# Softcap attention and a gated feed-forward layer: a fourth PSUM bank for the values, six early weight units, and a new order at the end of the first stage

## Chip, core and metric

The kernel runs on one NeuronCore of a Trainium2 chip. The metric is the device time of one execution in microseconds (us); the time given is the median of several executions. One execution was also profiled, and every row shown below comes from that one.

## What is computed

The input is an attention layer over 4 batches, 12 heads, 448 positions and 64 columns per head, with a cap on the scores, followed by a gated feed-forward layer over the 1792 rows that the attention gives (768 columns inside, 1536 in the middle). Everything is float32; the feed-forward weights arrive as 64-bit floats.

```python
scores = scale * np.matmul(q, k.transpose(0, 1, 3, 2))
scores = cap * np.tanh(scores / cap)
attn = np.exp(scores - np.max(scores, axis=-1, keepdims=True))
attn = attn / (np.sum(attn, axis=-1, keepdims=True) + 1e-09)
x = np.matmul(attn, v)                 # 4 x 12 x 448 x 64, then 1792 x 768
gate = 1.0 / (1.0 + np.exp(-(x @ w_gate)))
out = (gate * (x @ w_val)) @ w_out
```

## The kernel before

**Attention.** Heads are worked on in pairs: 24 pairs, six to a batch. For pair n the program transposes K and Q on TensorE (`tp`, L208), splits the result into a high and a low part (`T`: high by ScalarE, L175, low by VectorE, L181), multiplies them into four chunks of scores (`sc`, L323, six matmuls of each), takes the tanh of each chunk (ScalarE, L326) and one exp per head (L334). The values are multiplied in pair n+1's turn, one head at a time (`emit_PV`, tiles `pv`, L364, four matmuls of 448 columns each for one head). For the first twelve pairs ("direct") the row sums come out of the same matmuls, as a second half of the `pv` tile. ScalarE copies them into `rd` (L389, one buffer), and VectorE does the normalisation: it adds an epsilon (L413), takes the reciprocal (L414), and multiplies (L417, two instructions, which for the first six pairs read `pv` straight from PSUM). The result `xraw` is then split for the feed-forward layer into `xspl`, one slot per pair (`flush_x`: high by GpSimd, L173, low by GpSimd in batch 0 and by VectorE later, L181).

**PSUM.** There are eight banks: two tiles of two banks for scores and transposes (`ps_s`), one bank `ps_v`, and three banks `ps_m`. In the first stage, in which the first six pairs run with no feed-forward work beside them (`alone`), all `pv` tiles take turns in the three banks of `ps_m`, and `ps_v` lies unused. A pair needs two `pv` tiles, so the second one of a pair needs a bank that the pair before has just used, and which is free only when both L417 of that pair are done. From pair 6 on `pv` tiles use `ps_v`, and `ps_m` holds the feed-forward sums.

**Weights.** The feed-forward weights are 36 units of 768 KB: 0 to 23 are columns of w_gate and w_val in turns of four, 24 to 35 are rows of w_out. Each is loaded raw (L594), converted by one ScalarE (L611) and three VectorE instructions (L612 to L614) and split into high (L175 on ScalarE, or L173 on GpSimd for an early unit) and low (L181 on VectorE); the split unit `wspl` is written to memory (`wd`, L650) for the later batches. `o.early` units are converted in the first stage, in the order 3, 4, ..., 0, 1, 2, at a pace set by how much attention has been done (L819); the early ones from 3 on are loaded back when they are needed (L662). The others are converted in batch 0 of the feed-forward layer, unit u+4 when unit u begins.

**Feed-forward.** For each batch (`moe`): 24 tiles `h` (L706, 18 matmuls of 448 columns over six slots of `xspl`, in order of the slots, so the last three need pair 5 of the batch), then the output `o` (L782). While batch b's feed-forward work runs, the attention of batch b+1 is woven in: TensorE and ScalarE follow the program's order, and the loop at L826 hands out pieces of one or the other so that the done shares stay level, against a total of 570 for the feed-forward side (`tot_m`). The pieces of one batch's feed-forward work add up to 617 by their own weights (432 for the `h` tiles, 185 for the `o` tiles), so the attention of a batch is over before the feed-forward work is. On VectorE, GpSimd and the DMA queue of SyncE a scheduler sets the order when the program is built, by priority, which is program order unless a block raises it.

At the end of the first stage (n = 6, `last`), the loop L430 runs pair 6's first two score chunks, both heads' values of pair 5, pair 5's normalisation, and then leaves the stage; pair 6's other two chunks, pair 7's transposes and scores come as woven work:

```python
        for late in range(2):
            if (late == 0) != last and live:
                yield emit_S(n, 2) + emit_S(n, 3)
                emit_T(n + 1)
```

Of the kernel before, what the change touches and what calls it, by code (L numbers as in the profile page):

```python
# [20 lines left out]
EPS = 1e-9  # L21
WARM = 10
BANK = 512
NCH = 4

# [5 lines left out]
def tile_softcap_attention_then_gated_ffn(  # L31
# [33 lines left out]
    c["v0"] = c["pair0"][:, 2 * n0:].rearrange("p (c d) -> p c d", d=q.shape[3])  # L65
    _load_inside(nc.sync, c["qk0"][:, 1], k, 0)
    _load_inside(nc.scalar, c["qk0"][:, 0], q, 0)
    _load_evenly(nc, c["v0"], v, 0)
# [30 lines left out]

def _load_inside(eng, t, src, n):  # L100

    s = _pair(src, n)
    for h in range(2):
        eng.dma_start(
            out=t[0:src.shape[2] // NCH, :, h, :], in_=s[h].rearrange("(c p) d -> p c d", c=NCH)
        )
# [41 lines left out]
class _Ops:  # L148
# [37 lines left out]
    def load_qk(self, n, evenly=False):  # L186

        if n >= self.B * self.NPAIR:
            return None
        qk = self.ap.tile([P, 2, NCH, 2, self.D], F32, tag="qk", bufs=2, name=f"qk{n}")  # L190
        if evenly:
            _load_inside(self.nc.sync, qk[:, 1], self.k, n)
        else:
            _load_k(self.nc, qk[:, 1], self.k, n)
        _load_inside(self.nc.sync, qk[:, 0], self.q, n)
        return qk
# [18 lines left out]
def _bounded_attention(o, x_done):  # L215
# [14 lines left out]
    nc, c, ap = o.nc, o.c, o.ap  # L230
    o.early = 10
    o.out_tag = ("v_spl", 2)
# [123 lines left out]
    def emit_PV(n, j):  # L356
        if alone(n):
            pv = o.ps_m.tile([P, S], F32, tag="m", name=f"pv{n}_{j}")
        else:
            pv = o.ps_v.tile([P, S], F32, tag="v", name=f"pv{n}_{j}")  # L360
# [38 lines left out]
    def emit_out(n):  # L399
        b, p = divmod(n, o.NPAIR)  # L400
        xr = row(n)
        if direct(n):
            rd = rds.pop(n)
        else:
            ps = o.two_banks(f"dn{n}")[:, 0, 0:S]
            for j in range(2):
                nc.tensor.matmul(
                    ps, ones[:, (1 - j) * D:(3 - j) * D], Asum.pop((n, j)), start=(j == 0),
                    stop=(j == 1),
                )  # L410
            rd = ap.tile([P, S], F32, tag="rd", bufs=1, name=f"rd{n}")
            nc.scalar.activation(rd, ps, AF.Copy)
        nc.vector.scalar_tensor_tensor(rd, rd, EPS, rd, ALU.mult, ALU.add)  # L413
        nc.vector.reciprocal(rd, rd)  # L414
        if alone(n):
            for j in range(2):
                nc.vector.tensor_mul(xr[half(j)], pvs.pop((n, j))[0:D], rd[half(j)])  # L417
        else:
            nc.vector.tensor_mul(xr, xr, rd)
        x_done(b, p, x_raw[b])  # L420

# [6 lines left out]
    for n in range(NP + 1):  # L428
# [3 lines left out]
        if n > 0:  # L432
# [3 lines left out]
            if not direct(n - 1):  # L436
                emit_P(n - 1, 1)
        for late in range(2):

            if (late == 0) != last and live:  # L440
                yield emit_S(n, 2) + emit_S(n, 3)
                emit_T(n + 1)
                if n + 2 < NP:
                    qks[n + 2] = o.load_qk(n + 2, direct(n + 2))
                yield 5
                emit_exp(n, 0)
                if not direct(n):
                    emit_P(n, 0)
            if late != last and n > 0:
                yield from emit_PV(n - 1, 1)  # L450
# [4 lines left out]
                yield 2  # L455
                vs.pop(n - 1)
                if n % o.NPAIR == 0:
                    yield None
                load_v(n + 1)
        if not live:  # L460
# [87 lines left out]
def _emit(tc, ctx, c, attention_of, q, k, v, w_gate, w_val, w_out, out):  # L548
# [265 lines left out]
    with tc.manual_schedule(engines=MS):  # L814
# [6 lines left out]
        for b in range(B):  # L821
            m = moe(b)
            done_m, done_a, tot_m, tot_a = 0, 0, 570, H * o.head(b + 1)
            live_a = b + 1 < B
# [44 lines left out]
```

## Time and profile before

| | |
|---|---|
| median of 3 runs | 808.39 us (807.21 to 809.38) |
| the profiled execution | 810.49 us |
| its span, first to last instruction | 808.7 us |
| TensorE busy | 761.1 us (94%) |
| VectorE busy | 463.5 us (57%) |
| ScalarE busy | 398.1 us (49%) |
| GpSimd busy | 200.8 us (25%) |
| granted TensorE clock, mean | 0.972 |

The time of an execution is the span and a little around it (1.79 us here). Busy shares are means over very different stages: the first stage ends at about 104 us, feed-forward batch 0 at about 296 us, and the end of the span has no attention in it. Clock 1.0 is 2.4 GHz, 0.5 is 1.2 GHz.

### The profile page before, as it was taken

How to read it: one execution, taken by the hardware profiler on the slowest of the kernel's cores; microseconds unless marked ns; L12 is line 12 of the kernel's file. 1: busy time of each engine (PE TensorE's matmuls, PEld its weight loads, DVE VectorE, ACT ScalarE, POOL GpSimd, SP SyncE). 2: the span in 40 equal slices, each digit the busy share in tenths (PEclk: the TensorE clock that was granted, in tenths of full speed). 3: DMA queues.
4: the chain of work that ended last, by engine and by line, in shares of the span. 5: the costliest groups of instructions: out<-in, count | busy, mean ns of one | idle time of the engine just before them, and what ended most of it. 6: DMA issues, size and time to landing. Idle time of an engine off the chain costs nothing.

```text
span 808.7 us, 10161 instructions
## 1 busy us (share of the span) xinstructions
PE 761.1 (94%) x3908; PEld 647.6 (80%) x3908; DVE 463.5 (57%) x519; ACT 398.1 (49%) x417; POOL 200.8 (25%) x215
## 2 busy tenths in 40 slices
PE   7988789999998989999999999999998999999993
PEld 5544468878777878898889898889898999999993
DVE  1699803769798972865788545677688101211000
ACT  5787446676865654757574428565852020110000
POOL 1233301002030050634355322445363000100000
PEclk8999989999999998999999999999999999999997
DMA  9599675688999994566557776454469866665531
GB/s 224 155 291 285 201 234 160 204 259 276 346 307 300 351 286 144 183 194 188 171 184 228 246 246 194 167 184 156 157 192 272 284 245 219 232 211 200 174 110 53
DMA packets 133745, 176.14 MB, mean 218 GB/s; under 512 B 86200, under 2 KB 111288, under 8 KB 133688
## 3 DMA queue, kind: packets, MB, share of 16 engines
q1 hardware_dynamic: 132760, 175.17, 67.6%
q8 instruction: 33, 0.54, 0.3%
q10 hardware_dynamic: 928, 0.23, 0.1%
q14 instruction: 24, 0.20, 0.1%
HBM read 138.41 MB, written 36.18 MB: 216 GB/s over the span
## 4 chain that ended last, share of the span: by engine, by line
PE 73%; DVE 12%; ACT 5%; POOL 4%; issue 3%; DMA 1%; SPq 0%; POOLq 0%; DVEq 0%; ACTq 0%
PE h L706 39%; PE o L782 17%; PE pv L364 6%; PE sc L323 6%; DVE rd L414 3%; PE pv L373 2%; PE pv L374 2%; PE tp L208 1%; DVE pl L181 1%; POOL xspl L173 1%; ACT ph L175 1%; ACT gate L744 1%; DVE rd L413 1%; PE tp L294 1%; DVE ph L181 1%
## 5 line engine op out<-in xcount | busy, mean ns | idle before, releaser
L706 PE MATMUL h<-xspl,wspl 128*128 128x448 f32 x1728 | 380.2, 374 | 10.9 <-POOL xspl L181 6.5
L706 PEld LDWEIGHTS h<-xspl,wspl 128*128 128x128 f32 x1728 | 323.5, 189 | 53.7 <-issue 14.2
L782 PE MATMUL o<-wspl,gspl 128*128 128x384 f32 x864 | 161.2, 339 | 3.3 <-DVE osb L795 1.9
L782 PEld LDWEIGHTS o<-wspl,gspl 128*128 128x128 f32 x864 | 150.5, 188 | 9.4 <-issue 3.5
L326 ACT ACTIVATE t<-sc,scale 112x896 f32<-112x896 f32 (+1 forms) x96 | 91.2, 1001 | 25.5 <-PE sc L323 25.0
L173 POOL TENSOR_SCALAR gspl<-gate 128x448 fp32r<-128x448 f32 x48 | 39.2, 816 | 222.9 <-DVE gate L740 222.9
L364 PE MATMUL pv<-t,vo 112*128 112x448 f32 x192 | 86.3, 586 | 5.7 <-DVE xraw L417 5.7
L738 ACT ACTIVATE gate<-h 128x448 f32<-128x448 f32 x48 | 25.9, 542 | 124.0 <-PE h L706 98.4
L334 ACT ACTIVATE t<-t,capv 112x1792 f32<-112x1792 f32 (+1 forms) x48 | 85.6, 1788 | 0.4
L323 PE MATMUL sc<-T 64*112 64x448 f32 (+1 forms) x576 | 75.6, 392 | 5.2 <-ACT T L175 2.0
L323 PEld LDWEIGHTS sc<-T 64*112 64x112 f32 (+1 forms) x576 | 49.9, 183 | 30.8 <-issue 12.4
L414 DVE RECIPROCAL rd<-rd 128x448 f32<-128x448 f32 x24 | 70.8, 2948 | 0.4
L740 DVE TENSOR_TENSOR gate<-h,gate 128x448 f32<-128x448 f32 x48 | 29.3, 611 | 68.9 <-PE h L706 68.8
L364 PEld LDWEIGHTS pv<-t,vo 112*128 112x128 f32 x192 | 37.9, 204 | 36.1 <-issue 31.0
L181 DVE TENSOR_TENSOR T<-tp,T 128x896 fp32r<-128x896 f32 (+1 forms) x24 | 26.8, 1118 | 58.2 <-ACT T L175 58.2
L346 POOL TENSOR_TENSOR a<-t 128x448 f32<-128x448 f32 x24 | 29.8, 1243 | 117.2 <-ACT t L334 102.1
L797 ACT ACTIVATE osb<-o 128x384 f32<-128x384 f32 x8 | 3.9, 491 | 101.8 <-PE o L782 89.0
L795 DVE COPY osb<-o 128x384 f32<-128x384 f32 x16 | 8.7, 551 | 71.7 <-PE o L782 71.6
L181 DVE TENSOR_TENSOR pl<-t,ph 128x1344 fp32r<-128x1344 f32 x24 | 46.3, 1928 | 4.3 <-ACT ph L175 4.2
L175 ACT ACTIVATE ph<-t 128x1792 fp32r<-128x1792 f32 x24 | 40.7, 1696 | 14.3 <-PE pv L375 11.3
L175 ACT ACTIVATE T<-tp 128x896 fp32r<-128x896 f32 (+1 forms) x24 | 22.7, 944 | 43.2 <-PE tp L208 43.2
L181 DVE TENSOR_TENSOR gspl<-gate,gspl 128x448 fp32r<-128x448 f32 x48 | 31.3, 653 | 17.4 <-POOL gspl L173 16.6
(68 smaller groups left out, 758.8 us busy)
## 6 DMA issues: line engine op xcount, KB each, us to landing
wspl<-wd SPq DMA_DIRECT2D x115, 768.0 KB, 4.4
wd<-wspl SPq DMA_DIRECT2D x36, 768.0 KB, 6.4
w<-in_moe_w_gate_dram SPq DMA_DIRECT2D x12, 768.0 KB, 5.2
w<-in_moe_w_val_dram SPq DMA_DIRECT2D x12, 768.0 KB, 7.1
w<-in_moe_w_out_dram SPq DMA_DIRECT2D x12, 768.0 KB, 7.2
qk<-in_q_dram SPq DMA_DIRECT2D x46, 112.0 KB, 4.3
out_dram<-osb SPq DMA_DIRECT2D x8, 576.0 KB, 6.4
qk<-in_k_dram SPq DMA_DIRECT2D x22, 112.0 KB, 3.9
```

Source lines behind the costliest of these rows:

```text
L173: self.nc.gpsimd.tensor_scalar(dst, src, 1.0, 1.0, ALU.mult, ALU.mult)
L175: self.nc.scalar.activation(dst, src, AF.Copy)
L181: e.tensor_sub(dst, src, hi.bitcast(F32))
L323: nc.tensor.matmul(ps[0:w, j, 0:S], a[rows], r[rows], start=(i == 0), stop=(i == len(ops) - 1))
L326: nc.scalar.activation(Pt[n][0:w, :, m, :], ps[0:w, :, 0:S], AF.Tanh, scale=c["scale"][0:w])
L334: nc.scalar.activation(t, t, AF.Exp, scale=c["cap"][rows])
L346: nc.gpsimd.tensor_add(a, t[:, 0, :], t[:, 1, :])
L364: nc.tensor.matmul(pv, vs[n][0:QC, j * NC + m, :], Pt[n][0:QC, j, m, :], start=(m == 0), stop=(m == NC - 1),)
L414: nc.vector.reciprocal(rd, rd)
L706: nc.tensor.matmul(ps, a, r, start=(kk == 0 and i == 0), stop=(kk == KD - 1 and i == 2))
L740: nc.vector.tensor_mul(gt, ps, gt)
L782: nc.tensor.matmul(ps, a, r, start=(x + kk == 0 and i == 0), stop=(x + kk == KF - 1 and i == 2),)
```

## The change

Six edits. The first loads of K and Q are shared between the queues of SyncE and ScalarE by head. Six units are early instead of ten. In the first stage the second head's `pv` of an even pair goes to `ps_v`, so that four banks take turns. The normalisation, from L413 to the split into `xspl`, stands in a block of higher priority for the scheduler of VectorE, GpSimd and the SyncE queue. At n = 6 the stage does pair 6's last score chunks, pair 7's transposes and the loads of pair 8 before it ends. `tot_m` goes from 570 to 545, so that attention is handed out faster.

```diff
+AHEAD_OF = 400
...
-    _load_inside(nc.sync, c["qk0"][:, 1], k, 0)
-    _load_inside(nc.scalar, c["qk0"][:, 0], q, 0)
+    for src, i in ((k, 1), (q, 0)):
+        _load_inside((nc.sync, nc.scalar), c["qk0"][:, i], src, 0)
...
-        eng.dma_start(
+        engines[h % len(engines)].dma_start(
...
-    o.early = 10
+    o.early = 6
...
-        if alone(n):
+        if alone(n) and not (j == 1 and n % 2 == 0):
             pv = o.ps_m.tile([P, S], F32, tag="m", name=f"pv{n}_{j}")
         else:
             pv = o.ps_v.tile([P, S], F32, tag="v", name=f"pv{n}_{j}")
...
-        nc.vector.scalar_tensor_tensor(rd, rd, EPS, rd, ALU.mult, ALU.add)
-        nc.vector.reciprocal(rd, rd)
-        if alone(n):
-            for j in range(2):
-                nc.vector.tensor_mul(xr[half(j)], pvs.pop((n, j))[0:D], rd[half(j)])
-        else:
-            nc.vector.tensor_mul(xr, xr, rd)
-        x_done(b, p, x_raw[b])
+        with o.tc.high_priority(offset=AHEAD_OF):
+            nc.vector.scalar_tensor_tensor(rd, rd, EPS, rd, ALU.mult, ALU.add)
+            nc.vector.reciprocal(rd, rd)
+            if alone(n):
+                for j in range(2):
+                    nc.vector.tensor_mul(xr[half(j)], pvs.pop((n, j))[0:D], rd[half(j)])
+            else:
+                nc.vector.tensor_mul(xr, xr, rd)
+            x_done(b, p, x_raw[b])
...
-        for late in range(2):
-
-            if (late == 0) != last and live:
-                yield emit_S(n, 2) + emit_S(n, 3)
-                emit_T(n + 1)
-                if n + 2 < NP:
-                    qks[n + 2] = o.load_qk(n + 2, direct(n + 2))
-                yield 5
-                emit_exp(n, 0)
-                if not direct(n):
-                    emit_P(n, 0)
-            if late != last and n > 0:
+        first = n == o.NPAIR
+        if first:
+            yield from emit_PV(n - 1, 1)
+            emit_rd(n - 1, 0)
+            emit_rd(n - 1, 1)
+            emit_out(n - 1)
+        if live:
+            yield emit_S(n, 2) + emit_S(n, 3)
+            emit_T(n + 1)
+            if n + 2 < NP:
+                qks[n + 2] = o.load_qk(n + 2, direct(n + 2))
+            yield 5
+            if first:
+                yield None
+            emit_exp(n, 0)
+            if not direct(n):
+                emit_P(n, 0)
+        if n > 0:
+            if not first:
                 yield from emit_PV(n - 1, 1)
...
-            done_m, done_a, tot_m, tot_a = 0, 0, 570, H * o.head(b + 1)
+            done_m, done_a, tot_m, tot_a = 0, 0, 545, H * o.head(b + 1)
```

How the engines' orders move is shown at three places. In a row the tile's name carries its pair (or batch and number), then a running number; the last column is the shape and the count. Rows of the changed kernel carry its own line numbers, which are one to nine higher.

On TensorE, at the end of the first stage, the program before stands so from pair 6's transposes on:

```order
L208 MATMUL tp6_645<-ident_58,qk6_561 128x112 x8
L364 MATMUL pv4_1_663<-t4_500,vo4_496 128x448 x4
L323 MATMUL sc6_0_682<-T6_654 112x448 x6
L323 MATMUL sc6_1_690<-T6_654 112x448 x6
L364 MATMUL pv5_0_709<-t5_596,vo5_592 128x448 x4
L364 MATMUL pv5_1_714<-t5_596,vo5_592 128x448 x4
L323 MATMUL sc6_2_742<-T6_654 112x448 x6
L323 MATMUL sc6_3_750<-T6_654 112x448 x6
L706 MATMUL h0_0_0_762<-xspl0_301,wspl0_638 128x448 x18
L208 MATMUL tp7_781<-ident_58,qk7_657 128x112 x8
```

and after the change, from the values of pair 5 on:

```order
L365 MATMUL pv5_0_665<-t5_563,vo5_559 128x448 x4
L365 MATMUL pv5_1_670<-t5_563,vo5_559 128x448 x4
L324 MATMUL sc6_2_695<-T6_610 112x448 x6
L324 MATMUL sc6_3_703<-T6_610 112x448 x6
L209 MATMUL tp7_711<-ident_58,qk7_613 128x112 x8
L324 MATMUL sc7_0_734<-T7_720 112x448 x6
L324 MATMUL sc7_1_742<-T7_720 112x448 x6
L715 MATMUL h0_0_0_754<-xspl0_301,wspl0_541 128x448 x18
```

Pair 7's transposes and its first two score chunks now stand ahead of the first feed-forward tile, where they stood behind it.

On VectorE, the normalisations of pairs 4 and 5 with the conversions of units 1 and 2 (`w64_1`, `w64_2`; `wspl1`, `wspl2` are their low parts) stood so before:

```order
L417 TENSOR_TENSOR xraw0_296<-pv4_1_663,rd4_668 64x448
L612 TENSOR_SCALAR pair0_67<-pair0_67 128x768 x2
L613 SCALAR_TENSOR_TENSOR pair0_67<-w64_1_531,pair0_67 128x768
L613 SCALAR_TENSOR_TENSOR pair0_67<-w64_2_581,pair0_67 128x768
L614 SCALAR_TENSOR_TENSOR pair0_67<-w64_1_531,pair0_67 128x768
L614 SCALAR_TENSOR_TENSOR pair0_67<-w64_2_581,pair0_67 128x768
L413 SCALAR_TENSOR_TENSOR rd5_730<-rd5_730 128x448
L181 TENSOR_TENSOR wspl1_702<-pair0_67,wspl1_702 128x768
L414 RECIPROCAL rd5_730<-rd5_730 128x448
L181 TENSOR_TENSOR wspl2_723<-pair0_67,wspl2_723 128x768
L417 TENSOR_TENSOR xraw0_296<-pv5_0_709,rd5_730 64x448
```

and stand so after:

```order
L182 TENSOR_TENSOR wspl1_622<-pair0_67,wspl1_622 128x768
L419 TENSOR_TENSOR xraw0_296<-pv4_0_580,rd4_635 64x448
L419 TENSOR_TENSOR xraw0_296<-pv4_1_630,rd4_635 64x448
L621 TENSOR_SCALAR pair0_67<-pair0_67 128x768
L622 SCALAR_TENSOR_TENSOR pair0_67<-w64_2_461,pair0_67 128x768
L623 SCALAR_TENSOR_TENSOR pair0_67<-w64_2_461,pair0_67 128x768
L415 SCALAR_TENSOR_TENSOR rd5_686<-rd5_686 128x448
L416 RECIPROCAL rd5_686<-rd5_686 128x448
L182 TENSOR_TENSOR wspl2_679<-pair0_67,wspl2_679 128x768
L182 TENSOR_TENSOR T7_720<-tp7_711,T7_720 128x2x448
L419 TENSOR_TENSOR xraw0_296<-pv5_0_665,rd5_686 64x448
L419 TENSOR_TENSOR xraw0_296<-pv5_1_670,rd5_686 64x448
```

Ahead of a pair's normalisation there is now one unit's conversion where there were two, and pair 7's low part T7 stands ahead of pair 5's multiplications.

On TensorE, at the end of feed-forward batch 0, pair 11 is the last pair that batch 1 needs. Before, its last two value matmuls stood 12 output matmuls ahead of the batch's end (o0_1_1 and o0_1_2 of unit 35), which pair 13's scores and batch 1's first tile follow:

```order
L364 MATMUL pv11_1_2250<-t11_1770,vo11_1766 128x448 x2
L782 MATMUL o0_1_1_2071<-wspl35_2178,gspl0_758 128x384 x6
L782 MATMUL o0_1_2_2072<-wspl35_2178,gspl0_758 128x384 x6
L323 MATMUL sc13_0_2302<-T13_2212 128x448 x6
L323 MATMUL sc13_1_2310<-T13_2212 128x448 x6
L706 MATMUL h1_0_0_2322<-xspl1_1796,wspl36_2183 128x448 x18
```

After the change they stand 66 ahead of it (11 rows of six), and the same scores and the same tile follow:

```order
L365 MATMUL pv11_1_2164<-t11_1690,vo11_1686 128x448 x2
L791 MATMUL o0_1_1_2087<-wspl32_2093,gspl0_750 128x384 x6
L791 MATMUL o0_1_2_2088<-wspl32_2093,gspl0_750 128x384 x6
L791 MATMUL o0_1_0_2086<-wspl33_2139,gspl0_750 128x384 x6
L791 MATMUL o0_1_1_2087<-wspl33_2139,gspl0_750 128x384 x6
L791 MATMUL o0_1_2_2088<-wspl33_2139,gspl0_750 128x384 x6
L791 MATMUL o0_1_0_2086<-wspl34_2183,gspl0_750 128x384 x6
L791 MATMUL o0_1_1_2087<-wspl34_2183,gspl0_750 128x384 x6
L791 MATMUL o0_1_2_2088<-wspl34_2183,gspl0_750 128x384 x6
L791 MATMUL o0_1_0_2086<-wspl35_2215,gspl0_750 128x384 x6
L791 MATMUL o0_1_1_2087<-wspl35_2215,gspl0_750 128x384 x6
L791 MATMUL o0_1_2_2088<-wspl35_2215,gspl0_750 128x384 x6
```

The last units 33 to 35 of batch 0 run with no attention between them, and what stands between pair 11's values and batch 1's first tile has grown by 54 matmuls.

## Rows read from the trace of the kernel before

**Rows 1.** Windows: length, busy us (count) of each engine, clock, DMA share, GB/s.
```profile
26.00:105.00 79.00, 63.94 (x266) 34.93 (x267) 69.79 (x69) 56.35 (x59) 27.91 (x28) 0.91 0.81 251
105.00:204.00 99.00, 99.00 (x483) 79.37 (x482) 58.26 (x71) 64.25 (x74) 10.00 (x11) 0.98 0.71 222
204.00:300.00 96.00, 91.70 (x473) 75.57 (x472) 82.59 (x97) 65.93 (x74) 17.98 (x18) 1.00 0.94 317
```

**Rows 2.** Waits of TensorE, 0 to 110 us: total, times, longest.
```profile
PE h L706 <- POOL xspl L181: 6.5, 1, 6.5
PE pv L364 <- DVE xraw L417: 5.7, 4, 2.1
```

**Rows 3.** Timeline of TensorE: start, length, engine, line, operation, count, wait before it.
```profile
6.19 0.96 PE L208 MATMUL tp<-ident,pair 112*128 112x112 f32 x8 [0.20 <-DMA pair<-in_k_dram]
...
30.26 1.60 PE L323 MATMUL sc<-T 64*112 64x448 f32 x12
...
40.99 0.45 PE L323 MATMUL sc<-T 64*112 64x448 f32 x2
...
43.15 3.27 PE L364 MATMUL pv<-t,vo 112*128 112x448 f32 x8
...
50.47 4.97 PE L364 MATMUL pv<-t,vo 112*128 112x448 f32 x8 [1.17 <-DVE xraw L417]
...
81.47 1.48 PE L323 MATMUL sc<-T 64*112 64x448 f32 x12
...
94.14 3.31 PE L706 MATMUL h<-xspl,wspl 128*128 128x448 f32 x15
103.92 0.74 PE L706 MATMUL h<-xspl,wspl 128*128 128x448 f32 x1 [6.46 <-POOL xspl L181]
```

**Rows 4.** Groups of VectorE by line, 26 to 105 us: busy us, mean ns.
```profile
L414 DVE RECIPROCAL rd<-rd 128x448 f32<-128x448 f32 x6 | 17.7, 2944 | 0.1
L614 DVE SCALAR_TENSOR_TENSOR pair<-w,pair 128x768 uint16<-128x768 uint32 x10 | 11.9, 1202 | 0.1
L613 DVE SCALAR_TENSOR_TENSOR pair<-w,pair 128x768 int32<-128x768 int32 x10 | 10.9, 1097 | 0.2
L181 DVE TENSOR_TENSOR wspl<-pair,wspl 128x768 fp32r<-128x768 f32 x10 | 9.8, 982 | 2.3 <-POOL wspl L173 2.3
L417 DVE TENSOR_TENSOR xraw<-pv,rd 64x448 f32<-64x448 f32 x12 | 7.4, 613 | 0.2
L612 DVE TENSOR_SCALAR pair<-pair 128x768 int32<-128x768 int32 x10 | 5.8, 593 | 11.2 <-ACT pair L611 11.1
L181 DVE TENSOR_TENSOR T<-tp,T 128x896 fp32r<-128x896 f32 x5 | 5.4, 1077 | 0.0
L413 DVE SCALAR_TENSOR_TENSOR rd<-rd 128x448 f32<-128x448 f32 x6 | 4.3, 721 | 1.3 <-ACT rd L389 1.2
```

**Rows 5.** Groups of ScalarE by line, 26 to 105 us: busy us, mean ns.
```profile
L326 ACT ACTIVATE t<-sc,scale 112x896 f32<-112x896 f32 x22 | 20.9, 1003 | 6.3 <-PE sc L323 6.1
L334 ACT ACTIVATE t<-t,capv 112x1792 f32<-112x1792 f32 x10 | 17.9, 1788 | 0.1
L611 ACT ACTIVATE pair<-w 128x768 f32<-128x768 f32 x10 | 9.0, 901 | 0.6 <-DVE wspl L181 0.6
L389 ACT ACTIVATE rd<-pv 64x448 f32<-64x448 f32 x12 | 6.5, 541 | 9.9 <-PE pv L364 9.3 <-DVE xraw L417 0.4
L175 ACT ACTIVATE T<-tp 128x896 fp32r<-128x896 f32 x5 | 4.6, 916 | 0.7 <-PE tp L208 0.7
```

**Rows 6.** Groups of GpSimd by line, 26 to 105 us: the split of xraw.
```profile
L181 POOL TENSOR_TENSOR xspl<-xraw,xspl 128x448 fp32r<-128x448 f32 x6 | 8.8, 1460 | 0.5
L173 POOL TENSOR_SCALAR xspl<-xraw 128x448 fp32r<-128x448 f32 x6 | 6.0, 1002 | 28.5 <-DVE xraw L417 28.5
```

**Rows 7.** The page's group of the output matmuls: busy us, mean ns.
```profile
L782 PE MATMUL o<-wspl,gspl 128*128 128x384 f32 x864 | 161.2, 339 | 3.3 <-DVE osb L795 1.9
```

**Rows 8.** Timeline of TensorE where batch 1 of the feed-forward layer begins.
```profile
304.56 3.73 PE L706 MATMUL h<-xspl,wspl 128*128 128x448 f32 x9 [4.48 <-DVE xspl L181]
```

More of the change, by code (lines that the diff above doesn't have):

```diff
@@ L97, in _pair, with _load_inside @@
     return src[b, 2 * p:2 * p + 2]
-def _load_inside(eng, t, src, n):
+def _load_inside(engines, t, src, n):
     s = _pair(src, n)
     for h in range(2):
-        eng.dma_start(
+        engines[h % len(engines)].dma_start(
             out=t[0:src.shape[2] // NCH, :, h, :], in_=s[h].rearrange("(c p) d -> p c d", c=NCH)
@@ L191, in load_qk @@
         if evenly:
-            _load_inside(self.nc.sync, qk[:, 1], self.k, n)
+            _load_inside([self.nc.sync], qk[:, 1], self.k, n)
         else:
             _load_k(self.nc, qk[:, 1], self.k, n)
-        _load_inside(self.nc.sync, qk[:, 0], self.q, n)
+        _load_inside([self.nc.sync], qk[:, 0], self.q, n)
         return qk
@@ L455, in _bounded_attention @@
                 yield 2
[L456 to L459, printed above, removed]
+            vs.pop(n - 1)
+            if n % o.NPAIR == 0 and not first:
+                yield None
+            load_v(n + 1)
         if not live:
```

## The prediction

> **What bounds the kernel now.** I read the windows first. TensorE has 79 us between 26 and 105 us and is busy for 63.94 of them, while VectorE is busy for 69.79; from 105 to 204 us TensorE is busy all the time (99.00 of 99.00), and from 204 to 300 us for 91.70 of 96 [rows 1] (the columns are length, then busy time and count of TensorE, its weight loads, VectorE, ScalarE and GpSimd, then clock, DMA share, GB/s). So only the first stage has much to give, and there the busiest engine is VectorE.
>
> The waits say what ends last in the stage: one wait of 6.5 us of the first feed-forward tile for GpSimd's split of pair 5, and four waits, 5.7 us together, of a `pv` matmul for L417, that is for a PSUM bank [rows 2]. The timeline shows what a bank wait costs. Pair 2's first scores start at 30.26, pair 3's at 40.99, with no bank wait between: a period of 10.73 us. Pair 6's start at 81.47, so the next three periods took 40.48 us together, 13.49 each. The cost is more than the wait: after a wait of 1.17 us the eight `pv` matmuls took 4.97 us, where 3.27 is usual [rows 3]. The granted clock over the whole stretch is 0.91 [rows 1], so slowed matmuls of this kind are a part of what a wait costs.
>
> Why L417 is late: VectorE is busy for 69.79 us of 79, and ten units' conversions are 10 x (0.593 + 1.097 + 1.202 + 0.982) = 38.7 us of that [rows 1, 4]. They stand between the steps of the normalisation.
>
> The second place is the start of feed-forward batch 1: after 15 matmuls TensorE waits 4.48 us for pair 11's low part, and the nine matmuls behind it take 3.73 us [rows 8], while 15 unhindered ones took 3.31, so nine take 1.99 [rows 3].
>
> **The change part by part.**
>
> *Fewer early units, priority, fourth bank: the periods.* With six units over six pairs VectorE has one unit a pair: 3.87 us of conversion, 1.08 for T, 0.72 + 2.94 + 2 x 0.61 for the normalisation, 9.83 us in all [rows 4]. ScalarE has 4 x 1.00 + 2 x 1.79 + 0.92 + 2 x 0.54 + 0.90 = 10.48 us [rows 5]. Both are below the 10.73 us that a period takes when TensorE runs through. With four banks a pair's second `pv` takes a bank from two pairs back instead of one, so the wait has a whole period of slack. I take 10.73 for each of the three periods: 40.48 - 32.19 = 8.29 us less. ScalarE's 10.48 is close; that is the least safe part of this term.
>
> *The end of the stage.* Count from the start of pair 6's first scores. T6's low part is done 1.27 us earlier (the transposes are followed by 3.27 us of `pv`, and T takes 0.92 + 1.08) [rows 3 to 5]. VectorE then does, in the new order, unit 1's three steps (2.89, to 1.6), pair 4's L413 and L414 (to 5.3), the low part of unit 1 (to 6.3), two L417 (to 7.5); `rd` is free and ScalarE copies pair 5's sums beside unit 2's three steps (to 10.4); L413, L414 of pair 5 (to 14.0), unit 2's low part (to 15.0), T7 (to 16.1), two L417 (to 17.3) [rows 4]. GpSimd's split adds 1.00 + 1.46 (to 19.8) [rows 6]. TensorE meanwhile does 1.48 of scores, 2 x 3.27 of `pv`, 1.48 and about 1.0 of pair 6's other scores and pair 7's transposes, two matmuls of pair 7's scores, and then waits for T7 at 16.1; the ten that are left take 1.3 and the tile's first 15 matmuls 3.31, so the 16th, the one that waited before, comes at 20.7 [rows 3]. GpSimd is done by then: the 6.5 us wait is gone, and a wait of some 3.7 us for T7 has taken its place. Before, the 16th came at 103.92 - 81.47 = 22.45 [rows 3]. That is 1.75 us less, and 1.48 + 0.96 = 2.44 us of pair 7's work, which came later before, is done by then [rows 3]. Both have a slow patch of matmuls behind the wait; I set the one against the other. First stage: 8.29 + 1.75 + 2.44 = 12.5 us.
>
> *The moved units.* Units 6 to 9 are now converted while the first tiles run. That is 4 x 3.87 = 15.5 us more for VectorE, which had 58.26 of 99 busy, and 4 x 0.90 for L611 and about as much for the splits (estimated at L611's duration, the same 128x768) for ScalarE, which had 64.25; TensorE never waited there [rows 1, 4, 5]. A unit is converted four units before it is used, with 18 x 3.31 / 15 = 3.97 us of matmuls to a unit [rows 3]. Four raw loads and four writes of 768 KB move in and four reloads fall away, 3.1 MB on top of 222 GB/s x 99 us = 22 MB at a DMA share of 0.71 [rows 1]. I price it at nothing; the cover is that slack. If it were gone the bound is the 4.3 us that TensorE loses from 204 to 300 us, where VectorE has 82.59 of 96 busy with the same conversions [rows 1].
>
> *570 to 545.* Pair 11's last value matmul now has 66 output matmuls, 12 score matmuls and 15 of the new tile ahead of the one that needs it: 66 x 161.2 / 864 + 1.48 + 3.31 = 17.1 us [rows 3, 7]. Before it was 12 x 0.187 + 4.79 = 7.0 and TensorE waited 4.48 more [rows 7, 8], so the chain takes 11.5. It is covered: 4.48 + (3.73 - 1.99) = 6.2 us less. The price is attention that is denser by 570 / 545, 4.6%, elsewhere. Where VectorE has slack it costs nothing; from 204 to 300 us I charge 1.0 us, between 0 and that stretch's whole 4.3 [rows 1].
>
> *The first loads.* K's two halves are issued on two queues at once, and Q's last half takes the place that K's had on SyncE. The first transposes waited 0.20 us for K [rows 3], so I take 0.2, between 0 and 0.2. The Trainium skill (DMA: Bandwidth & Descriptors, Issuing engines are not separate DMA queues) says that all queues run on the same 16 DMA engines and that using several saves only the time to issue; the wait is of that order. If K and Q arrive no earlier the term is 0 and the sum 0.2 us worse.
>
> *Sum.* 12.5 + 6.2 + 0.2 - 1.0 = 17.9 us. The profiled execution took 810.49 us, so 792.6; the median of the runs lies 2.10 below that execution, and the same difference gives 790.5.
>
> **The rivals.**
>
> *VectorE stays the bound.* GpSimd's split follows directly on L417, and T and the next unit's conversion run beside it. If they are held up by all of its 2.46 us [rows 6], VectorE needs 9.83 + 2.46 = 12.3 us a pair, above 10.73: three periods lose 1.56 each and the end of the stage 2.46, 7.1 us in all, 797.6. For it: L613 and L614, near twins, average 1.10 and 1.20 us in this stretch. Against it: the means of rows 4 already contain what collisions there were. The Trainium skill (SBUF — State Buffer, Who interferes with whom) says that a VectorE instruction with two SBUF inputs and a GpSimd one that reads SBUF shut each other out, the later one waiting for the whole of the earlier; by it this rival is what happens wherever both fall together, and no row here shows how often.
>
> *The boundary gain is eaten.* If units 32 to 35, which now run without attention between them, wait for their conversions, or the denser attention makes the stretch to 300 us wait by as much as batch 1 gains, 6.2 us go: 796.7. For it: VectorE at 82.59 of 96 there. Against it: the conversions are handed out by units, and they get more time per unit until the attention ends.
>
> *Slower.* The first feed-forward tiles wait for units 6 to 9: the raw load comes too late, and a conversion lies on the path: 0.90 + 2.89 + 0.90 + 0.98 = 5.7 us a unit, 22.7 us for four [rows 4, 5], which takes the 17.9 and 4.8 more: 813.2. It decides once a raw load lands more than the lead of some 16 us, less 5.7, after its issue: 10 us. A DMA share of 0.71 speaks against that [rows 1].
>
> *Nothing to see.* The single `rd` buffer takes the place of the bank: ScalarE's copy of a pair's sums waits for L417 of the pair before, and the tanh behind it waits too. If that keeps the periods at 13.49 and the boundary gain is eaten as well, 17.9 - 8.3 - 6.2 = 3.4 less the end of the stage's 1.75: 806.7. By the count above `rd` is free before a pair's sums are ready or at most 0.5 us after.
>
> *Better.* TensorE's 4.3 us from 204 to 300 us vanish too, because normalisations no longer stand behind conversions, and nothing is charged: 785.2.
>
> **How the numbers follow.** Forecast 0.62; VectorE stays the bound 0.14; boundary eaten 0.10; better 0.06; nothing to see 0.04; slower 0.04. The range from 784 to 800 takes in the first four, with the bounds of the charges. A difference of 0.3% (2.4 us) is about what a measurement of this kernel can tell from no change; faster than that are the first four cases, 0.92, within it 0.04, slower 0.04.
>
> **What would show it.** In the changed kernel no `pv` wait for L417 should be left, pairs' first scores should start 10.5 to 11.2 us apart, all `pv` pairs of eight should take about 3.3 us, and the first tile should start near 89 to 91 us and run through its 16th matmul with at most 1 us of wait; a wait of 3 to 4 us for T7 should stand ahead of it. From there to 200 us TensorE should not wait. At batch 1's start no wait for the low part should stand, and the window that reaches there should end about 18 us earlier. The prediction is wrong if periods stay near 13 us (then the bank was not what bound them), or if a stall of the same size stands behind the boundary or in the stretch of the w_out units.

## The result, and the profile after

| | before | after |
|---|---|---|
| median of 6 runs each | 808.88 us (806.84 to 810.58) | 801.7 us (799.72 to 804.3) |
| profiled execution, its span | 810.49, 808.7 us | 801.68, 799.9 us |

The ratio is 0.9915 [0.9891, 0.9938]: the change gains 7.2 us. The forecast was 790.5 us with a range from 784 to 800, so the time lies outside it, on the slow side.

The windows of the changed kernel answer to [rows 1] (same columns). The two windows behind the three are the places where the kernel now loses time.

```profile
26.00:105.00 79.00, 71.54 (x331) 43.33 (x330) 54.06 (x53) 60.71 (x64) 19.79 (x24) 0.96 0.70 200
105.00:204.00 99.00, 98.61 (x480) 78.51 (x478) 80.14 (x96) 76.28 (x87) 9.12 (x12) 1.00 0.87 282
204.00:300.00 96.00, 85.98 (x431) 73.59 (x430) 79.06 (x90) 51.51 (x60) 20.87 (x20) 0.95 0.82 285
250.00:290.00 40.00, 31.46 (x156) 28.00 (x156) 32.33 (x35) 18.55 (x23) 7.52 (x6) 0.87 0.80 301
585.00:612.00 27.00, 22.57 (x115) 21.52 (x114) 24.18 (x26) 7.68 (x8) 14.13 (x15) 0.94 0.81 222
```

In the first stage TensorE is busy for 7.6 us more of the 79, and VectorE for 15.7 us less. But from 204 to 300 us, where the sum charged 1.0 us, TensorE is busy for 5.7 us less than before, and its granted clock is 0.95 instead of 1.00. In the kernel before, the 40 us that end just ahead of batch 1, as 250 to 290 us do in the changed kernel, look so:

```profile
256.00:296.00 40.00, 40.00 (x212) 33.80 (x212) 33.54 (x38) 25.63 (x30) 7.03 (x7) 1.00 0.98 342
```

Before, TensorE ran through there, at a granted clock of 1.00. Now it is busy for 31.46 of 40 us, at 0.87. The waits of TensorE say for what. From 0 to 110 us (total, times, longest):

```profile
PE sc L324 <- DVE T L182: 5.6, 3, 4.3
PE tp L209 <- ACT t L327: 3.1, 7, 0.9
```

Both rows of [rows 2] are gone. And from 110 to 800 us:

```profile
PE o L791 <- DVE wspl L182: 5.3, 1, 5.3
PE tp L295 <- ACT t L327: 4.9, 5, 1.8
PE pv L374 <- DVE xraw L398: 4.4, 1, 4.4
PE o L791 <- ACT osb L806: 3.0, 1, 3.0
```

The timeline of TensorE in the changed kernel puts them in their places. The profile shows each value matmul (`pv`) of the first twelve pairs as two; the counts of matmuls here are those of the profile.

```profile
58.36 1.47 PE L324 MATMUL sc<-T 64*112 64x448 f32 x12
...
68.88 1.48 PE L324 MATMUL sc<-T 64*112 64x448 f32 x12
70.28 6.28 PE L365 MATMUL pv<-t,vo 112*128 112x448 f32 x16
...
85.62 2.21 PE L324 MATMUL sc<-T 64*112 64x448 f32 x10 [4.31 <-DVE T L182]
87.76 5.15 PE L715 MATMUL h<-xspl,wspl 128*128 128x448 f32 x18
...
257.84 2.29 PE L791 MATMUL o<-wspl,gspl 128*128 128x384 f32 x6 [3.02 <-ACT osb L806]
...
264.61 3.66 PE L791 MATMUL o<-wspl,gspl 128*128 128x384 f32 x18
...
269.27 8.86 PE L791 MATMUL o<-wspl,gspl 128*128 128x384 f32 x48
283.44 5.68 PE L791 MATMUL o<-wspl,gspl 128*128 128x384 f32 x18 [5.31 <-DVE wspl L182]
289.05 1.49 PE L324 MATMUL sc<-T 64*128 64x448 f32 x12
290.47 5.12 PE L715 MATMUL h<-xspl,wspl 128*128 128x448 f32 x24
...
598.29 0.44 PE L374 MATMUL pv<-pl,vs 128*128 128x448 f32 x1 [4.43 <-DVE xraw L398]
```

Pairs 5 and 6 start their scores 10.52 us apart; the first feed-forward tile starts at 87.76 and runs through its 18 matmuls. Batch 1's first tile (290.47) takes all its matmuls from `xspl1` without a wait, where before there were 4.48 us [rows 8]. But ahead of it stand 48 output matmuls without attention, then 5.31 us of waiting for unit 35's low part, and 18 matmuls that take 5.68 us, where 18 at 264.61 took 3.66.

**Where the lead went.** I compare the starts of the same matmuls in the two profiled executions. The first output matmul starts at 222.2 instead of 234.7 us, and by then eight `pv` matmuls and twelve score matmuls more are done (168 and 288 instead of 160 and 276), which take 3.21 and 1.40 us in the first stage (28.22 and 26.82): a lead of 12.5 + 4.6 = 17.1 us. Batch 1's first tile starts at 290.47 instead of 296.72, a lead of 6.25. So 10.8 us are lost between 222 and 290. Behind the next 24 matmuls (that tile's 18 and six of the second) and seven value matmuls of pair 12 the lead is 13.55 (296.84 instead of 310.39): the boundary gave 7.3. Batch 3's first tile starts at 635.52 instead of 644.17, a lead of 8.65, so 4.9 more are lost; the largest wait on the way is the one at 598.29. To the end of the span nothing changes (8.8).

**Why unit 35 is late.** VectorE's timeline in the changed kernel, ahead of the wait:

```profile
271.90 0.86 DVE L621 TENSOR_SCALAR pair<-pair 128x768 int32<-128x768 int32 x1
...
275.92 0.94 DVE L622 SCALAR_TENSOR_TENSOR pair<-w,pair 128x768 int32<-128x768 int32 x1
276.79 2.94 DVE L416 RECIPROCAL rd<-rd 128x448 f32<-128x448 f32 x1
...
280.41 1.02 DVE L623 SCALAR_TENSOR_TENSOR pair<-w,pair 128x768 uint16<-128x768 uint32 x1
...
282.34 1.05 DVE L182 TENSOR_TENSOR wspl<-pair,wspl 128x768 fp32r<-128x768 f32 x1 [0.41 <-ACT wspl L176]
```

Unit 35's L621, L622, L623 and low part take 3.87 us in themselves and stand spread over 11.5 us, from 271.90 to 283.39, with a reciprocal and other steps of attention between them. VectorE does these without a pause; TensorE, with no attention left to do, arrives early at the unit and waits.

### The profile page after: what moved, and what is told of

Its sections match the earlier page's. It is cut to its first block, busy times and chain, and to the rows that moved or that the text cites. A ratio compares the mean times of both kernels' runs of the same rounds, so it can differ in the third digit from the quotient of the medians.

```text
span 799.9 us, 10153 instructions
## 1 busy us (share of the span) xinstructions
PE 754.3 (94%) x3908; PEld 646.6 (81%) x3908; DVE 469.4 (59%) x519; ACT 401.3 (50%) x421; POOL 194.5 (24%) x211
## 4 chain that ended last, share of the span: by engine, by line
PE 68%; DVE 14%; ACT 8%; issue 4%; DMA 3%; POOL 1%; SPq 0%; DVEq 0%; POOLq 0%; ACTq 0%
PE h L715 32%; PE o L791 17%; PE pv L365 6%; PE sc L324 5%; DMA w<-in_moe_w_out_dram 2%; DVE pair L623 2%; PE tp L209 2%; ACT t L327 2%; DVE wspl L182 2%; PE pv L374 1%; ACT ph L176 1%; DVE rd L416 1%; PE pv L375 1%; DVE gspl L182 1%; ACT gate L753 1%
## 5 line engine op out<-in xcount | busy, mean ns | idle before, releaser
L791 PE MATMUL o<-wspl,gspl 128*128 128x384 f32 x864 | 164.4, 345 | 9.4 <-DVE wspl L182 5.3
L791 PEld LDWEIGHTS o<-wspl,gspl 128*128 128x128 f32 x864 | 154.5, 193 | 14.9 <-DVE wspl L182 5.6
L174 POOL TENSOR_SCALAR gspl<-gate 128x448 fp32r<-128x448 f32 x48 | 34.7, 723 | 206.4 <-DVE gate L749 202.4
L324 PE MATMUL sc<-T 64*112 64x448 f32 (+1 forms) x576 | 75.7, 392 | 9.4 <-DVE T L182 5.6
L365 PE MATMUL pv<-t,vo 112*128 112x448 f32 x192 | 78.6, 542 | 0.0
L365 PEld LDWEIGHTS pv<-t,vo 112*128 112x128 f32 x192 | 35.4, 189 | 25.2 <-issue 24.7
L182 DVE TENSOR_TENSOR gspl<-gate,gspl 128x448 fp32r<-128x448 f32 x48 | 37.8, 787 | 24.3 <-POOL gspl L174 23.9
L182 DVE TENSOR_TENSOR pl<-t,ph 128x1344 fp32r<-128x1344 f32 x24 | 48.2, 2009 | 4.6 <-ACT ph L176 3.9
L621 DVE TENSOR_SCALAR pair<-pair 128x768 int32<-128x768 int32 x36 | 21.0, 582 | 42.7 <-ACT pair L620 42.6
```

The lines of the kernel that those rows point to most:

```text
L174: self.nc.gpsimd.tensor_scalar(dst, src, 1.0, 1.0, ALU.mult, ALU.mult)
L182: e.tensor_sub(dst, src, hi.bitcast(F32))
L324: nc.tensor.matmul(ps[0:w, j, 0:S], a[rows], r[rows], start=(i == 0), stop=(i == len(ops) - 1))
L365: nc.tensor.matmul(pv, vs[n][0:QC, j * NC + m, :], Pt[n][0:QC, j, m, :], start=(m == 0), stop=(m == NC - 1),)
L791: nc.tensor.matmul(ps, a, r, start=(x + kk == 0 and i == 0), stop=(x + kk == KF - 1 and i == 2),)
```

## The experiments

Each kernel was timed beside the kernel before on the same chip; the medians of before there were 808.05 to 808.4 us. Ratios are to the kernel before; the change itself stands at 0.9915 [0.9891, 0.9938].

**Theory A: the denser attention (545) takes back the gain. Rival B: the priority of the normalisation does, by putting conversions late.** First, the changed kernel with 570.

```diff
-            done_m, done_a, tot_m, tot_a = 0, 0, 545, H * o.head(b + 1)
+            done_m, done_a, tot_m, tot_a = 0, 0, 570, H * o.head(b + 1)
```

> The changed kernel with 570 in place of 545, all else as changed (about 801.7 us with 545). Theory A, the denser attention brings TensorE to unit 35 and to the last pairs of batch 2 before VectorE has their work ready: the wait for the low part of unit 35 (5.3 us and slow matmuls behind it) and most of the wait for the last pair of batch 2 (4.4 us) go, a wait at the start of batch 1 may come back, but smaller than 4.5 us because attention has a head start: 793 to 797 us. Theory B, the priority of the normalisation delays conversions and batch 2's last pairs: both waits stay, 800 to 803 us.

Measured: 795.62 us (792.95 to 800.09), 0.9844 [0.9809, 0.9879], 6.1 us below the changed kernel. Its largest waits from 110 to 800 us:

```profile
PE pv L365 <- ACT xraw L392: 2.2, 1, 2.2
PE tp L295 <- ACT t L327: 2.1, 1, 2.1
PE o L791 <- DVE gate L749: 1.9, 1, 1.9
```

The wait for unit 35 and the one of 4.4 us for L398 are gone, and no wait for pair 11 has come back. The timeline of this kernel says why not:

```profile
281.89 6.78 PE L791 MATMUL o<-wspl,gspl 128*128 128x384 f32 x36
290.03 5.24 PE L715 MATMUL h<-xspl,wspl 128*128 128x448 f32 x24
```

With 570, and the rest of the change, 36 output matmuls already stand behind the last attention work of batch 0; with the scores and 15 matmuls of the tile they take 6.78 + 1.49 + 3.3 = 11.6 us, and the chain takes the 11.5 that the prediction worked out. The moved scores had put pair 11 far enough ahead. So of the 54 output matmuls by which pair 11's values moved, 24 are the moved scores' (36 instead of 12 behind them with 570) and 30 are 545's.

But the start of batch 1 shows more: the first tile starts at 290.03 us here and at 290.47 in the changed kernel. With 570 the wait for unit 35 is gone, and TensorE is still hardly earlier; it waits 1.93, 2.16 and 2.08 us between 223 and 272 us instead (this execution was also some 3 us slower near its start, which is told further below). In these two executions nearly all of the difference comes later: 4.43 us of wait at 598.29 have become 1.06.

Then the changed kernel without the block of priority (the lines in it stay as they are):

```diff
-        with o.tc.high_priority(offset=AHEAD_OF):
...
```

> The changed kernel without the block of higher priority. Theory A: both late waits stay, and the first stage may lose up to 2 us of what it gained: 801 to 805 us. Theory B: both late waits go and the time falls by 8 to 13 us, to 789 to 794 us.

Measured: 803.13 us (801.62 to 806.07), 0.9939 [0.9917, 0.9961]. The late waits stay:

```profile
PE o L790 <- DVE wspl L182: 5.2, 1, 5.2
...
PE pv L374 <- DVE xraw L398: 4.5, 1, 4.5
```

Rival B falls: the waits are there without the priority. The priority is worth 1.4 us by the medians, with overlapping intervals.

**545 alone, in the kernel before.** It has the boundary wait that 545 is to remove.

```diff
-            done_m, done_a, tot_m, tot_a = 0, 0, 570, H * o.head(b + 1)
+            done_m, done_a, tot_m, tot_a = 0, 0, 545, H * o.head(b + 1)
```

> The kernel before with 545 alone (about 808.9 us with 570). Theory A: batch 1's wait of 4.5 us shrinks, and waits in batch 0's output and at the end of batch 2 come: no gain, 808 to 814 us. Theory B: the boundary gain comes alone, 802 to 804 us.

Measured: 813.24 us (811.59 to 814.12), 1.0059 [1.0038, 1.0081]: slower. Some of its waits from 110 to 800 us:

```profile
PE tp L294 <- ACT t L326: 6.7, 5, 2.6
PE pv L373 <- DVE xraw L397: 4.2, 1, 4.2
...
PE h L706 <- DVE xspl L181: 1.0, 1, 1.0
```

The boundary wait falls from 4.48 to 1.0 us, where the prediction had none left (42 output matmuls stand behind pair 11's values here, not 66), and the denser attention loses more than that: TensorE's waits ahead of the transposes are 6.7 us in all, where the kernel before had one of 2.2, and the wait of 4.2 at the end of batch 2 comes with 545 in this kernel too (1.1 before).

**What made the first stage faster: the bank, or fewer conversions?** The changed kernel with three banks:

```diff
-        if alone(n) and not (j == 1 and n % 2 == 0):
+        if alone(n):
```

> The changed kernel with three banks for the values again. If the bank is what shortened the first stage, waits of the value matmuls for L417's successor come back and the pairs' scores start 12 to 13.5 us apart: the first tile starts 5 to 8 us later than 87.8 us. If fewer conversions did it, L417 is early enough for three banks, the period stays within 0.5 us of 10.5, and the time within 2 us of 801.7.

Measured: 805.32 us (801.72 to 807.08), 0.9963 [0.9943, 0.9982], 3.6 us above the changed kernel. Its waits from 0 to 110 us have the bank again, at less than half of [rows 2]:

```profile
PE pv L365 <- DVE xraw L419: 2.5, 3, 2.1
```

Its timeline shows pair 2's and pair 6's first scores and the first tile:

```profile
28.59 1.48 PE L324 MATMUL sc<-T 64*112 64x448 f32 x12
...
71.66 1.48 PE L324 MATMUL sc<-T 64*112 64x448 f32 x12
...
91.37 4.90 PE L715 MATMUL h<-xspl,wspl 128*128 128x448 f32 x14
```

Periods are 43.07 / 4 = 10.77 us with three banks, against 10.51 with four; the same four took (81.47 - 30.26) / 4 = 12.80 in the kernel before [rows 3]. Most of that way is covered without the bank. The largest bank wait left, 2.1 us, stands behind the last period. Of the 3.6 us by which the first tile comes later than in the changed kernel, 1.8 stand ahead of pair 2 already (28.59 instead of 26.82).

The changed kernel with ten early units:

```diff
-    o.early = 6
+    o.early = 10
```

> The changed kernel with ten early units again (all else as changed, 545 too; about 801.7 us with six). If VectorE's conversions were what held the first stage, the pairs' scores go from 10.5 to 11 us or more apart and the first tile starts 3 to 8 us later: 804 to 809 us. If priority and the fourth bank are enough, the period stays within 0.3 us and the time within 2 us of 801.7.

Measured: 812.35 us, 1.0057 [1.0035, 1.0079]. The trace shown is of the next run of the same kernel.

> The changed kernel with ten early units, once more for a trace at the usual clock (its median was 812.4 us, 10.6 above six units). If the cost is VectorE's load in the first stage, the pairs' scores stand 12 to 13 us apart, waits for T or for the bank are back, and the first tile starts 6 to 10 us after 87.8. If the stage is as short as with six units, the cost lies later, at batch 0's end, and waits there exceed the 5.3 + 3.0 us of the changed kernel.

Measured: 811.84 us, 1.0027 [1.0003, 1.0051], so ten early units cost about 10 us, more than was expected. Its largest wait from 0 to 110 us:

```profile
PE sc L324 <- DVE T L182: 12.5, 7, 4.9
```

Its timeline, with the first scores of pairs 2 and 6 and the first tile:

```profile
28.93 1.61 PE L324 MATMUL sc<-T 64*112 64x448 f32 x12
...
75.35 0.45 PE L324 MATMUL sc<-T 64*112 64x448 f32 x2
78.72 1.27 PE L324 MATMUL sc<-T 64*112 64x448 f32 x10 [2.92 <-DVE T L182]
...
99.28 4.44 PE L715 MATMUL h<-xspl,wspl 128*128 128x448 f32 x18
```

With four banks no `pv` waits, and the periods are still 46.42 / 4 = 11.6 us on average: VectorE, with ten units to convert, is late with T instead. The first tile comes 11.5 us later than in the changed kernel, 2.1 of them ahead of pair 2. So the bank wait looks like one form that VectorE's lateness took.

Six early units alone, in the kernel before:

```diff
-    o.early = 10
+    o.early = 6
```

> The kernel before with six early units and nothing else. If VectorE's conversions were the bound of the first stage, the pairs' scores stand 10.5 to 11 us apart with three banks and without priority, and the time is 798 to 802 us. If the bank or the priority is needed too, the bank waits stay and the time is 805 to 809 us.

Measured: 804.42 us (800.41 to 805.94), 0.9945 [0.992, 0.9969]. The first tile starts at 85.86 instead of 94.14 and its 16th matmul at 92.76 instead of 103.92, 8.3 and 11.2 us earlier. The first scores of pairs 2 and 6 stand 43.05 / 4 = 10.76 us a pair apart, with three banks and no priority, so fewer early units alone are enough for the period. But the edit gains only 4.4 us in all, between the two ranges expected: at 140 us it leads by 11.8, at 162 by 5.9. Its timeline at pairs 2 and 6 and at the place of that loss, and its wait at batch 1's start:

```profile
29.78 1.48 PE L323 MATMUL sc<-T 64*112 64x448 f32 x12
...
72.83 1.47 PE L323 MATMUL sc<-T 64*112 64x448 f32 x12
...
149.25 1.75 PE L208 MATMUL tp<-ident,qk 112*128 112x112 f32 x8 [2.59 <-ACT t L326]
...
299.61 3.73 PE L706 MATMUL h<-xspl,wspl 128*128 128x448 f32 x9 [4.49 <-DVE xspl L181]
```

ScalarE's tanh for that pair stands behind conversions which themselves wait for VectorE (1.48 and 2.80 us, at 145.55 and 142.80). So the moved units are not free everywhere. In the changed kernel the largest wait of this kind there is 0.40 us; I did not test what spares it.

**Where does 545 cost, and is unit 35's wait VectorE's order?** The denser attention in batch 0 alone:

```diff
-            done_m, done_a, tot_m, tot_a = 0, 0, 545, H * o.head(b + 1)
+            done_m, done_a, tot_m, tot_a = 0, 0, 545 if b == 0 else 570, H * o.head(b + 1)
```

> The changed kernel with 545 in batch 0 and 570 after it. Theory A says that 545 costs at two places, about 5 us of it at the end of batch 2 (the wait of 4.4 us for the last pair and slow matmuls behind it) and 1 to 4 us in batch 0: 796 to 798 us, with the wait for unit 35 left and the one for the last pair back to some 1 us. If the cost of 545 is all in batch 0: 800 to 803 us.

Measured: 798.13 us (797.18 to 802.57), 0.9896 [0.9872, 0.992], 3.6 us below the changed kernel. The wait of 4.4 us at batch 2's end is gone, the one for unit 35 is 4.5. By the medians 3.6 us of the 6.1 are lost after batch 0 and the rest in it; the intervals of this run and of 570 throughout overlap a little.

The changed kernel with conversions five units ahead of their use instead of four, and the split into high and low three instead of two:

```diff
-    AHEAD = 2
+    AHEAD = 3
...
-    LEAD = 4
+    LEAD = 5
```

> The changed kernel (545) with every unit converted and split one unit earlier: unit 35's conversion then stands ahead of pair 12's low parts and pair 11's reciprocal on VectorE. If it is that place in VectorE's order that makes TensorE wait for unit 35, the wait of 5.3 us goes or falls under 1 us, and the time by 4 to 7 us, to 795 to 798 us; batch 2's wait stays. If the raw load or the copies of the outputs bound it, the wait stays or moves, 800 to 803 us.

Measured: 796.99 us (794.16 to 800.38), 0.9873 [0.9847, 0.9899], 4.7 us below the changed kernel. Its timeline ahead of batch 1:

```profile
269.00 11.98 PE L791 MATMUL o<-wspl,gspl 128*128 128x384 f32 x66
282.34 5.22 PE L715 MATMUL h<-xspl,wspl 128*128 128x448 f32 x24
```

All 66 output matmuls run through in 11.98 us, and batch 1 starts 8.1 us earlier than in the changed kernel, with the same 545. That shows unit 35's wait as one of when its conversion stands in the engines' queues: with an earlier place it vanishes, though VectorE has the same work. The wait of 4.2 us at the end of batch 2 remains.

**Both remedies.** Lead five with 570 throughout:

```diff
-    AHEAD = 2
+    AHEAD = 3
...
-    LEAD = 4
+    LEAD = 5
...
-            done_m, done_a, tot_m, tot_a = 0, 0, 545, H * o.head(b + 1)
+            done_m, done_a, tot_m, tot_a = 0, 0, 570, H * o.head(b + 1)
```

> The same with 570. If density was the trouble in both batches and the longer lead adds slack, 791 to 795 us, at or under the 795.6 us of 570 alone; if the longer lead crowds VectorE or the loads, 796 to 800 us.

Measured: 796.51 us (794.52 to 798.1), 0.9857 [0.9837, 0.9876]: no better than 570 alone. And lead five with 545 in batch 0 alone:

```diff
-    AHEAD = 2
+    AHEAD = 3
...
-    LEAD = 4
+    LEAD = 5
...
-            done_m, done_a, tot_m, tot_a = 0, 0, 545, H * o.head(b + 1)
+            done_m, done_a, tot_m, tot_a = 0, 0, 545 if b == 0 else 570, H * o.head(b + 1)
```

> The changed kernel with the longer lead of the conversions, 545 in batch 0 and 570 after it. If the three costs are separate, the longer lead takes away unit 35's wait (4.7 us of the time) and 570 the wait of batch 2's last pair (3.6 us): 792 to 795 us, the fastest of all. If they overlap, no better than 795.6 us.

Measured: 792.36 us (790.53 to 793.53), 0.9799 [0.9774, 0.9824], the fastest: 9.3 us below the changed kernel. Its largest wait from 110 to 800 us:

```profile
PE o L791 <- ACT osb L806: 3.3, 1, 3.3
```

Its interval lies below that of lead five with 570 throughout, and overlaps that of 570 alone by a little.

So with the longer lead 545 in batch 0 gains 4.2 us over 570, while with the lead of four it lost about 2.5 (798.13 against 795.62, with overlapping intervals). The traces show the same in the stretch from the first output matmul of batch 0 to the 25th tile matmul of batch 1 (starts in us). Beside the kernel before, the changed kernels have done eight value matmuls more by the first of these (3.2 us, as above), and with 545 twelve score matmuls too (4.6 us together); the last column adds that work back.

| kernel | first output matmul | batch 1's first tile | batch 1's 25th tile matmul | stretch, at equal work |
|---|---|---|---|---|
| before | 234.66 | 296.72 | 310.39 | 75.7 us |
| changed: 545, lead four | 222.21 | 290.47 | 296.84 | 79.2 us |
| 570, lead four | 223.24 | 290.03 | 296.52 | 76.5 us |
| 570, lead five | 222.48 | 289.42 | 295.93 | 76.7 us |
| 545, lead five | 222.34 | 282.34 | 288.84 | 71.1 us |
| 545 in batch 0, lead five | 224.82 | 286.87 | 293.38 | 73.2 us |

With 570 the wait at the boundary is gone, and the stretch is no shorter than before: the time went in other waits ahead of it. Only 545 together with the longer lead makes it shorter, by 2.6 to 4.6 us. Four other executions with 545 in batch 0 and the lead of four give 77.1 to 80.1, so differences of 2 or 3 us in single executions say little.

## Why the prediction was wrong, point by point

**The failed step is "570 to 545".** Its words were: "Where VectorE has slack it costs nothing; from 204 to 300 us I charge 1.0 us, between 0 and that stretch's whole 4.3", against 6.2 us of gain at the boundary. Its net was a gain of 5.2 us; the runs put it at 6.1 us of loss (570 in the changed kernel) and about 5 (545 in the kernel before). Three things in it failed:
- The price was read from how busy VectorE was before, 82.59 of 96 us [rows 1], and the edit was charged as 4.6% more work in the same mould. What the edit did was to end the attention earlier. Then TensorE runs the last units at its own speed, and VectorE, which still has that attention's last steps in its queue, feeds them too late. The rows of the order shown ahead of the prediction had this stretch: units 33 to 35 with no attention between them. The prediction named it as a rival with a chance of 0.10 and the words "they get more time per unit until the attention ends" against it. Unit 35 was converted after the end, and the lead of five units shows that an earlier conversion removes the wait, for 4.7 us of the time. What was charged at 1.0 us was a loss of 10.8 in the profiled execution; not all of it is 545's, since with 570 some 8 us of lead go in the same stretch, through other waits that I did not trace further.
- It priced batch 0 only. The same constant rules the later batches, and by the medians 3.6 us were lost there (4.6 with the lead of five), most visibly in the wait of 4.43 us ahead of the last pair's values.
- It took the wait at the boundary for the gain. The wait went, and 7.3 us came back there, somewhat more than the 6.2 of the sum; but with 570 it is gone as well, because pair 7's scores and transposes, moved ahead of the first tile, pull the attention forward (six early units alone leave it at 4.49 us). Each edit was priced against the kernel before, not against the kernel with the other edits. And a wait that is gone is not yet time won: with 570 as much was lost ahead of the boundary. Where the conversions come one unit earlier, 545 in batch 0 does gain 4.2 us, near the 5.2 that the sum gave it; the sum lacked that condition.

The prediction's own sign of failure, "a stall of the same size stands behind the boundary or in the stretch of the w_out units", is what the trace shows.

**The first stage was right.** The sum had 12.5 us. At pair 7's work and the first tile the two executions are about 15 us apart at equal work; some 3 of these are luck of these two executions and not the change: near the start, ten score matmuls and the first eight `pv` matmuls took 2.21 and 5.35 us in that of before, and 1.27 and 3.27 in this one. Other kernels with the same start had 3.27 to 5.46 us for those eight. That leaves about 12. The periods are 10.51 us (forecast 10.73); the wait for T7 stands where it was put, 4.31 us instead of the forecast 3.7; GpSimd's split is done at 88.6 us, before the tile's 16th matmul; the first tile starts at 87.76, ahead of the 89 to 91 forecast.

**The cause within that stage was read half right.** The text put the bank wait and VectorE's conversions side by side. By the runs the conversions carry most: ten units back costs 10 us with the fourth bank in place, and six early units alone bring the period to 10.76 us in the kernel before; the bank back costs 3.6, the priority about 1.4 by the medians. The bank alone was not tried in the kernel before.

**The moved units cost nothing up to 222 us in the changed kernel**, as priced. The lead grew from about 15 to 17.1 us on the way, and TensorE was busy for 98.61 of the 99 us from 105 to 204. The run with six early units alone shows that this was not certain: there 5.9 us went between 140 and 162 us.

**The first loads**: the first transposes start at 5.48 instead of 6.19 us, 0.7 us earlier and without a wait, where the sum had 0.2. The issue of K's last half ends 0.53 us earlier (1.61 instead of 2.14 us). The warm-up matmuls ahead of the transposes took 4.29 us instead of 4.64, which is not the edit's: with the old loads they took 4.35 to 4.64 us, with the new ones 4.16 to 4.64. Over the kernels with the new loads the transposes start at 5.35 to 5.79 us, with the old ones at 6.08 to 6.19, so the edit gave 0.3 us or more; nothing here separates its two halves.

**"VectorE stays the bound"** did not come true as a bound, though its mechanism is seen. In the changed kernel L623 is once undisturbed and once falls beside GpSimd's split of `xraw`, which itself began while L622 ran. VectorE's timeline:

```profile
70.05 1.04 DVE L623 SCALAR_TENSOR_TENSOR pair<-w,pair 128x768 uint16<-128x768 uint32 x1
...
77.19 1.19 DVE L622 SCALAR_TENSOR_TENSOR pair<-w,pair 128x768 int32<-128x768 int32 x1
78.41 1.85 DVE L623 SCALAR_TENSOR_TENSOR pair<-w,pair 128x768 uint16<-128x768 uint32 x1
```

And GpSimd's at the same time:

```profile
77.66 1.72 POOL L182 TENSOR_TENSOR xspl<-xraw,xspl 128x448 fp32r<-128x448 f32 x1
```

The split alone takes 1.14 us (at 87.47). So each of the two lost some 0.6 to 0.8 us, and the periods had room for that. The Trainium skill (SBUF — State Buffer, Who interferes with whom) has a VectorE instruction with two SBUF inputs and a GpSimd one that reads SBUF shut each other out, the later one waiting for the earlier to end. These rows fit that: they fall together only in part, so each waits for the rest of the one before it. By the rule the split would end 1.14 us behind L622's end, at 79.52 (it ends at 79.38), and L623 1.04 us behind the split's, at 80.42 (80.26).

**What the sum became**, in the profiled executions: 17.1 up to 222 us, about 15 of them from the first stage (with some 3 from the slow start of the execution of before), less 10.8 to 290, plus 7.3 at the boundary, less 4.9 by batch 3, 8.8 us in all. The medians show 7.2.

**What stays open.** The wait of 4.0 to 4.3 us for T7 is in every kernel with the moved scores and six early units, with four banks, and I tried nothing against it. Why the changed kernel with 570 waits elsewhere ahead of batch 1, so that the boundary's gain is lost there, was not traced. That every kernel with 545 throughout loses 4.2 to 4.5 us ahead of the last pair's values, at the end of batch 2, was located and not traced further back. The moved scores and the edit of the first loads were not run alone.

## What to carry to other kernels

A constant that hands out filler work has two ends: handing it out faster brings the last result earlier, and leaves the tail of the main work with no filler, at its own full speed, against a feeder that still has the filler's last steps in its queue. Look at what the feeder does between the last filler and the end, in every batch the constant rules, before charging it as a percentage of work. And when several edits serve one wait, price each with the others already in place, and measure the gain as the lead at equal work on both sides of the place, not as the wait that went: here the same edit lost 2.5 us by the medians with the feeder four units ahead and gained 4.2 with it five units ahead.

## What the runs showed that I had not expected

A wait inside a busy stretch costs more than its length. After 5.31 us the next 18 output matmuls took 5.68 us instead of 3.66, after 3.02 us the next six took 2.29 against 1.31 for six that ran just before (at 251.98), and the granted clock of the window from 250 to 290 us was 0.87. So the wait of 5.31 us cost some 7.3. In the same way eight `pv` matmuls at the start of the kernel took from 3.27 to 5.46 us in different executions of kernels with the same matmuls ahead of them: 2 us of difference between two profiles can be this alone.
